# Two transformer layers on one core: output-side matmuls issued as four 128x32 column tiles, with a re-made instruction order and staging buffers in reused memory

## The chip, the cores and the metric

The kernel runs on one core of one Trainium2 chip. The metric is device time in microseconds (us), lower is better. A core has a matmul engine (PE, whose weight loads are shown as PEld), a vector engine (DVE), an activation engine (ACT), a general engine (POOL) and a queue engine (SP) that starts every data transfer (DMA) here. Each engine runs its own instruction list in order; semaphores tie the lists together.

## The reference

The input is one sequence of 2048 tokens of width 576 in bf16. The reference applies this twice:

```python
x = x + _A_ref(_layernorm(x), wqkv, wo)
x = x + _B_ref(_layernorm(x), w1, b1, w2, b2)
```

`_A_ref` normalizes again, makes q, k and v (32 heads of width 18), and does attention in which a token sees itself and the 255 tokens before it; the result goes through `wo` (576 by 576):

```python
mask = (idx[:, None] - idx[None, :] >= 0) & (idx[:, None] - idx[None, :] < W)   # W = 256
p = _softmax(jnp.where(mask, q @ k.T * Dh ** -0.5, -1e9))
o = p @ v
return o.reshape(B, S, D) @ wo
```

`_B_ref` normalizes, multiplies by `w1` (576 by 4608), applies gelu with bias `b1`, and multiplies by `w2` (4608 by 576), plus `b2`.

## The kernel before

Work is cut into 8 chunks: 4 per layer, each of 4 tiles of 128 tokens. Chunk k passes through these stages.

- **Normalization.** DVE makes statistics (L678, L682), POOL the reciprocal root (L691, L693), DVE the normalized tile `xn` (L703), and, for a 64-wide remainder of the 576 columns, a second copy of it (L711, DVE). A transposing DMA (L727) then makes `xnTa` (for attention) or `xnTm` (for the MLP). `xn` is a ring of 3 slots.
- **q, k, v.** In chunks 0 and 1 each of q, k and v of a tile is two groups of five 128-row matmuls with 288 columns (`two_out`, L763). In later chunks the array is split into two halves of 64 rows (L803), two matmuls of 288 columns running beside each other. Results leave PSUM, the matmul output memory of 8 banks, by DVE casts (L811 for v, L824 for q and k). Chunk 1 may use bank 6 alone for this.
- **Attention.** Scores (L870) use four row tiles of 32 rows (one head each); ACT takes the exponential (L879), POOL zeroes what the mask forbids (L900), and the product with v (L917, `pv`) uses four column tiles: each matmul has 128 rows and 20 of 32 columns and writes its own 32 partitions of one bank. DVE then transposes and normalizes (L928, L931, L934, L938).
- **Output projection** (`tail`, again L763): ten 128x128 matmuls per token tile with 288 columns, then the residual add on DVE (L980), and normalization for the MLP.
- **First MLP matmul** (`G_part`, L1033): pairs of 64-row matmuls with 512 columns; ACT applies gelu (L1043).
- **Second MLP matmul** (`mm2`, L1071): the 36 blocks of 128 hidden columns are done in three parts of 12; for each token tile and each half of 288 output columns, 12 matmuls with a 128x128 stationary block of `hT` accumulate in one bank, and DVE adds the result into `x_res` (L980), or, in the last part of layer 2, writes the output tile to a slot of `xn` (L983), from which a DMA sends it out.

So four ways of using the array occur: whole (128x128), two row halves (64x128), four row tiles (32x128) and four column tiles (128x32).

The order of all instructions is set at build time by a list scheduler in the kernel (`Plan.schedule`): a task has a cost, a priority and an array mode ("f" whole, "h" halves, "r" row tiles, "c" column tiles), a switch of mode costs a fixed time in its model, `PL.turn` adds a preference against certain switches, and `PL.nudge` shifts the priority of each stage by a table of constants. Chunks are interleaved: while chunk k is in attention, chunk k-1 is in the MLP. The scheduler also puts filler matmuls on a zeroed tile (L665) into planned gaps of the first 140 us.

Weights `w1` and `w2` are streamed from DRAM again for each chunk, through a ring of three slots (`w1_sb`) and one buffer (`w2_sb`) that is refilled in two loads per part (six blocks each).

Of the kernel before, what the change touches and what calls it, by code (L numbers as in the profile page):

```python
# [159 lines left out]
class Task:  # L160
    __slots__ = ("idx", "eng", "fn", "reads", "writes", "cost", "lat", "prio", "dma", "ring", "handles", "alloc", "move", "desc",
                 "npred", "succ", "ready", "end", "plain", "fifo", "hold", "stage", "mode", "own")
# [24 lines left out]
class Plan:  # L187
# [21 lines left out]
    def add(self, eng, fn, reads=(), writes=(), dma=None, ring=4, cost=0.1, lat=0.1, prio=0.0, alloc=(), fifo=None, plain=False, after=(), move=0.0, desc=0, hold=False, mode="f", own=False):  # L209
        if eng == "dve" and fifo is None:  # L210
# [5 lines left out]
                 plain=plain, move=move, desc=desc, fifo=fifo, hold=hold, stage=stage, mode=mode, own=own)  # L216
# [31 lines left out]
    def keep_warm(self, a, b, bank_free, extra):  # L248

        if self.warm_fn is None or a < self.warm_from:  # L250
            a = max(a, self.warm_from)
        n = int((b - a - 0.1) * 0.8 / 0.115)
        banks = [x for x in (7, 6, 5, 4) if bank_free.get(x, 1e9) <= a]
        if n < 1 or not banks:
            return
        h = Bank(())
        h.no = banks[0]
        t = Task(idx=-1, eng="pe", fn=lambda e: self.warm_fn(e, h.no, n), reads=("warm",), writes=(h,), cost=n * 0.115, lat=0.1, prio=0.0,
                 dma=None, ring=4, alloc=(), handles=(), plain=False, move=0.0, desc=0, fifo=None, hold=False, stage="", mode="f", own=False)
        extra.append((a, t))  # L260

    def schedule(self):
        free = {e: BEGIN for e in ENGS}
        mode = "f"
        released = {e: [] for e in ENGS}
# [152 lines left out]
def build_kernel(nc, A_x, A_wqkv, A_wo, B_x, B_w1, B_b1, B_w2, B_b2, out):  # L418
# [26 lines left out]
    NXN = 3  # L445
# [14 lines left out]
    PL.turn = {"ff": 0.02, "fh": 0.24, "fc": 0.44, "rf": 0.05, "rr": 0.16, "cf": 0.56, "ch": 1.05, "cr": 0.47, "cc": 0.72}  # L460
    PL.nudge = {"": -255.24, "b": -219.8, "ea0.0": 23.65, "ea0.1": -0.79, "ea0.2": 6.45, "ea0.p0": -38.42, "ea0.p1": 20.22,
# [803 lines left out]
```

## Time and profile before

| what | us |
|---|---|
| median of 3 runs (lowest, highest) | 881.62 (880.4, 881.86) |
| the profiled execution, whole time | 880.89 |
| span of that execution, first to last instruction | 879.2 |
| PE idle before 24 us / from 24 to 95 us | 2.3 / 6.7 |
| PE idle from 95 to 800 us / after 800 us | 6.2 / 2.9 |

The granted PE clock was 1.000 throughout. PE idle is the length of a stretch less PE's busy time in it; busy time includes the modelled end of a matmul, so it is an upper bound of useful work. The last matmul group starts at 864.38 us and is followed by the last residual add (876.35 us) and the last output transfer.

### The profile page before, as it was taken

How to read it: one execution, taken by the hardware profiler on the slowest of the kernel's cores; microseconds unless marked ns; L12 is line 12 of the kernel's file. 1: busy time of each engine (PE TensorE's matmuls, PEld its weight loads, DVE VectorE, ACT ScalarE, POOL GpSimd, SP SyncE). 2: the span in 40 equal slices, each digit the busy share in tenths (PEclk: the TensorE clock that was granted, in tenths of full speed). 3: DMA queues.
4: the chain of work that ended last, by engine and by line, in shares of the span. 5: the costliest groups of instructions: out<-in, count | busy, mean ns of one | idle time of the engine just before them, and what ended most of it. 6: DMA issues, size and time to landing. Idle time of an engine off the chain costs nothing.

```text
span 879.2 us, 23104 instructions
## 1 busy us (share of the span) xinstructions
PE 861.2 (98%) x9675; PEld 507.4 (58%) x9675; DVE 414.2 (47%) x994; ACT 596.3 (68%) x741; POOL 367.8 (42%) x500
## 2 busy tenths in 40 slices
PE   9898999999999999999999999999999999999998
PEld 7444555556566565566655555655556555556665
DVE  6889423664237632476433943374233533262111
ACT  5976788858757696565774868729768589753443
POOL 3766554465234562254420845416444176231100
PEclk9999999999999999999999999999999999999999
DMA  7698435361585524936356262584425953445341
GB/s 193 141 196 187 113 114 135 110 165 52 163 164 126 136 63 157 181 108 179 103 131 186 62 180 84 150 174 111 155 82 136 226 123 104 136 130 171 104 159 50
DMA packets 181847, 119.53 MB, mean 136 GB/s; under 512 B 107440, under 2 KB 181744, under 8 KB 181744
## 3 DMA queue, kind: packets, MB, share of 16 engines
q1 hardware_dynamic: 181744, 118.05, 52.0%
q8 instruction: 77, 1.26, 0.6%
q14 instruction: 26, 0.21, 0.1%
HBM read 90.10 MB, written 2.36 MB: 105 GB/s over the span
## 4 chain that ended last, share of the span: by engine, by line
PE 80%; DVE 7%; DMA 4%; ACT 4%; issue 3%; POOL 2%; SPq 0%; DVEq 0%; POOLq 0%
PE ps L1033 31%; PE ps L1071 28%; PE ps L803 9%; PE ps L870 5%; PE ps L917 4%; PE ps L763 4%; ACT pT L879 3%; DVE xn L703 2%; DMA xnTm<-xn 2%; POOL pT L900 1%; DVE st_all L678 1%; DVE xn L711 1%; DMA xnTa<-xn 1%; DVE x_res L980 1%; ACT hT L1043 1%
## 5 line engine op out<-in xcount | busy, mean ns | idle before, releaser
L900 POOL TENSOR_SCALAR_AFFINE_SELECT pT<-pT 128x512 bf16<-128x512 bf16 (+1 forms) x368 | 287.8, 805 | 271.6 <-ACT pT L879 267.9
L879 ACT ACTIVATE pT<-ps 128x1024 bf16<-128x1024 f32 (+2 forms) x384 | 347.1, 972 | 51.5 <-PE ps L870 51.1
L1071 PE MATMUL ps<-w_sb,hT 128*128 128x288 bf16 x2208 | 298.5, 287 | 3.8 <-DVE x_res L980 2.0
L1043 ACT ACTIVATE hT<-ps,b1col 128x512 bf16<-128x512 f32 x276 | 168.4, 688 | 195.3 <-PE ps L1033 194.6
L1033 PE MATMUL ps<-xnTm,w_sb 64*128 64x512 bf16 x2592 | 292.8, 376 | 0.2 <-ACT pT L879 0.2
L1071 PEld LDWEIGHTS ps<-w_sb,hT 128*128 128x128 bf16 x2208 | 203.2, 98 | 84.6 <-issue 23.7
L1033 PEld LDWEIGHTS ps<-xnTm,w_sb 64*128 64x128 bf16 x2592 | 126.9, 94 | 141.9 <-issue 6.7
L980 DVE TENSOR_TENSOR x_res<-ps,x_res 128x288 f32<-128x288 f32 x224 | 99.1, 446 | 170.1 <-PE ps L1071 136.3
L928 DVE STREAM_TRANSPOSE oq<-ps 128x512 f32<-128x512 f32 x64 | 45.6, 712 | 112.1 <-PE ps L917 111.5
L803 PE MATMUL ps<-wqkv,xnTa 64*128 64x288 bf16 x1296 | 95.4, 283 | 2.5 <-DMA xnTa<-xn 0.9
L824 DVE CAST qn<-ps 128x288 bf16<-128x288 f32 x120 | 49.7, 449 | 80.6 <-PE ps L803 72.5
L803 PEld LDWEIGHTS ps<-wqkv,xnTa 64*128 64x128 bf16 x1296 | 61.1, 94 | 35.0 <-issue 6.4
L870 PE MATMUL ps<-qT,kT 32*128 32x384 bf16 (+2 forms) x1216 | 64.1, 276 | 2.0 <-ACT pT L879 1.7
L691 POOL TENSOR_SCALAR vtmp<-mv_all 128x1 f32<-128x1 f32 (+1 forms) x43 | 8.8, 206 | 130.6 <-DVE mv_all L682 129.1
L1049 POOL TENSOR_TENSOR x_res<-x_res,b2bc 128x576 f32<-128x576 f32 x32 | 40.7, 1293 | 43.8 <-ACT hT L1043 43.8
L678 DVE BATCH_NORM_STATS2 st_all<-x_res 128x6 f32<-128x288 f32 (+1 forms) x128 | 53.7, 443 | 1.7 <-DMA x_res<-in_A_x_dram 1.2
L917 PE MATMUL ps<-pT,vA 128*20 128x384 bf16 (+2 forms) x1408 | 50.4, 276 | 1.0 <-DVE qn L824 0.8
L703 DVE TENSOR_SCALAR xn<-x_res,mv_all,rstd 128x576 bf16<-128x576 f32 (+1 forms) x64 | 43.8, 685 | 13.8 <-DMA xnTm<-xn 5.7
L811 DVE CAST vA<-ps 128x288 bf16<-128x288 f32 x64 | 26.5, 448 | 40.5 <-PE ps L803 38.5
L763 PE MATMUL ps<-wo_sb,attT 128*128 128x288 bf16 x320 | 44.2, 287 | 0.6 <-DVE x_res L980 0.6
L870 PEld LDWEIGHTS ps<-qT,kT 32*128 32x128 bf16 x1216 | 19.4, 92 | 43.1 <-issue 30.3
L917 PEld LDWEIGHTS ps<-pT,vA 128*20 128x20 bf16 x1408 | 25.8, 90 | 23.1 <-issue 11.6
(47 smaller groups left out, 389.7 us busy)
## 6 DMA issues: line engine op xcount, KB each, us to landing
w_sb<-in_B_w_dram SPq DMA_DIRECT2D x48, 864.0 KB, 5.9
w_sb<-in_B_w_dram SPq DMA_DIRECT2D x48, 768.0 KB, 4.7
w_sb<-in_B_w_dram SPq DMA_DIRECT2D x96, 48.0 KB, 4.4
out_dram<-xn SPq DMA_DIRECT2D x16, 144.0 KB, 1.8
wqkv<-in_A_wqkv_dram SPq DMA_DIRECT2D x3, 576.0 KB, 5.3
x_res<-in_A_x_dram SPq DMA_DIRECT2D x3, 576.0 KB, 4.3
wo_sb<-in_A_wo_dram SPq DMA_DIRECT2D x4, 144.0 KB, 3.3
xnTm<-xn SPq DMA_TRANSPOSE x32, 2.6
```

Of the source, the lines that this page charges most:

```text
L678: add("dve", lambda e, i=i, s=s: e.bn_stats(st_all[:, t, i, :], s[:, t, i * HB:(i + 1) * HB]), reads=res, writes=[f"st{t}_{i}"], cost=0.37 ...
L703: add("dve", lambda e: e.tensor_scalar(xn[:, sl, 0:D], s[:, t, :], mv_all[:, t, 0:1], rstd[:, t:t + 1], op0=ALU.subtract, op1=ALU.mult), r ...
L763: ins = e.matmul(bank(bs[o])[:, 0:HB], lhs(c), rhs(c, o * HB), start=(c == 0), stop=(c == KD - 1))
L803: ins = e.matmul(bank(bs[o])[:, 0:HB], xnTa[r:r + 64, c, i * 128:(i + 1) * 128], wqkv[r:r + 64, c, col:col + HB], start=(c == 4), stop=(ph ...
L870: ins = e.matmul(two(bs[j // 2])[:, j % 2, col:col + nq * 128], k_of(T0 + so)[0][32 * j:32 * j + 32, g, :], qs[32 * j:32 * j + 32, g, qo * ...
L879: add("act", lambda e, h2=h2: e.activation(pT[:, sl, 2 * h2:2 * h2 + 2, lo:hi], two(bs[h2])[:, :, lo:hi], ACT.Exp, scale=SCALE), reads=[bs ...
L900: add("pool", lambda e, ap=ap, pat=pat, sgn=sgn, kind=kind: e.affine_select(ap, ap, pattern=pat, compare_op=(ALU.is_ge if kind == "d" else ...
L917: ins = e.matmul(bank(bo)[32 * j:32 * j + VW, qo * 128:(qo + nq) * 128], vA[:, (T0 + so) % VS, 8 * j + g, :], pT[:, sl, j, col:col + nq * ...
L980: add("dve", lambda e: e.tensor_tensor(x_res[:, t, sl], bank(b)[:, 0:HB], x_old[:, t, sl], ALU.add), reads=[b] + ([f"xin{t}"] if first els ...
L1033: ins = e.matmul(bank(bks[i])[:, 0:n], w1_sb[r:r + 64, sls[i], col:col + 128], xnTm[r:r + 64, k % 2, c, 0:n], start=(c == 4), stop=(ph == ...
L1043: add("act", lambda e, ff=ff, hd=hd, bk=bk: e.activation(hd[:, 0:n], bank(bk)[:, 0:n], ACT.Gelu_apprx_tanh, bias=b1col[:, ff:ff + 1]), rea ...
L1071: ins = e.matmul(bank(b)[:, 0:HB], h_of(k, hf, fl)[0][:, i * 128:(i + 1) * 128], w2_sb[:, fl, hh * HB:(hh + 1) * HB], start=(fl == 0), sto ...
```

## The change

1. A helper `quad` issues one 128x128 by 288 product as four matmuls, each with 32 columns of the stationary block, the same moving operand, and its own 32 output partitions. It replaces the single matmul in the second MLP matmul, in the output projection, and in chunk 1's q, k and v. The scheduler's mode of these tasks becomes "c".
2. The scheduler's constants change: `PL.turn`, the whole `PL.nudge` table, several task costs, and a rule that DVE's two normalizing operations and POOL's work exclude each other in the plan ("port"). So the order on every engine is new.
3. The second copy of the 64-wide remainder of `xn` moves from DVE (a second normalization) to POOL (a copy). The ring of `xn` grows from 3 to 4 slots.
4. Chunk 1's q, k and v may use banks 6 and 7 instead of 6 alone.
5. In the first chunk of each layer the three score units of a head hold 384, 384 and 384 columns instead of 384, 512 and 256.
6. Dead space: 12 of the 16 output tiles are staged in `x_res` of tiles that are finished; the last chunk's last part of `w2` is loaded over `wqkv`; `b1` arrives in a block of `hT`; the filler's zero tile is half as wide.

```diff
     GW = GS * 128
-    NXN = 3
+    NXN = 4
...
-    PL.turn = {"ff": 0.02, "fh": 0.24, "fc": 0.44, "rf": 0.05, "rr": 0.16, "cf": 0.56, "ch": 1.05, "cr": 0.47, "cc": 0.72}
+    PL.turn = {"hc": 0.3, "rh": 0.05, "rc": 0.05, "ch": 0.3}
...
                 for t in released[e]:
                     st = max(free[e], t.ready)
+                    if t.port:
+                        st = max(st, port)
...
+            if t.port:
+                port = st + t.cost
...
-    b1in = sb("b1in", [NF, P], BF16)
+    b1in = hT[0:NF, NFH - 1, 0:P]
+    x_out = x_res[:, :, 0:HB].bitcast(BF16)
...
-            reads=res + [f"mv{t}", f"rstd{t}"], writes=[f"xn{sl}"], cost=0.67 if src is None else 0.45, lat=0.14, prio=prio)
+            reads=res + [f"mv{t}", f"rstd{t}"], writes=[f"xn{sl}"], cost=0.5 if src is None else 0.37, lat=0.14, prio=prio, port=True)
...
-            add("dve", lambda e: e.tensor_scalar(xn[:, sl, D:KD * 128], s[:, t, 512:D], mv_all[:, t, 0:1], rstd[:, t:t + 1],
-                                                  op0=ALU.subtract, op1=ALU.mult),
-                reads=res + [f"mv{t}", f"rstd{t}"], writes=[f"xd{sl}"], cost=0.38, lat=0.14, prio=prio)
+            add("pool", lambda e: e.tensor_copy(xn[:, sl, D:KD * 128], xn[:, sl, 512:D]), reads=[f"xn{sl}"], writes=[f"xd{sl}"], cost=0.22, lat=0.1,
+                prio=prio)
...
+    w2_x = wqkv.rearrange("p c d -> p (c d)")[:, 0:NFH * D].rearrange("p (f d) -> p f d", d=D)
+    def w2_of(k, hf):
+        return (w2_x, "w2x") if k == NK - 1 and hf == NPT - 1 else (w2_sb, "w2s")
...
+    def quad(e, b, lhs, rhs, start, stop):
+        ins = None
+        for j in range(4):
+            ins = e.matmul(bank(b)[32 * j:32 * j + 32, 0:HB], lhs[:, 32 * j:32 * j + 32], rhs, start=start, stop=stop,
+                           tile_position=(0, 32 * j), skip_group_check=True)
+        return ins
...
                 for c in range(KD):
-                    ins = e.matmul(bank(bs[o])[:, 0:HB], lhs(c), rhs(c, o * HB), start=(c == 0), stop=(c == KD - 1))
+                    if mode == "c":
+                        ins = quad(e, bs[o], lhs(c), rhs(c, o * HB), c == 0, c == KD - 1)
+                    else:
+                        ins = e.matmul(bank(bs[o])[:, 0:HB], lhs(c), rhs(c, o * HB), start=(c == 0), stop=(c == KD - 1))
...
-                             wr, prio + 0.01 * n, after=dest, fill=(6,) if k == 1 else FILL)
+                             wr, prio + 0.01 * n, after=dest, fill=(6, 7) if k == 1 else FILL, mode="c" if k == 1 else "f")
...
+        if t0 == 0:
+            us = [[(0, 0, 3, 0)], [(1, 1, 3, 128)], [(2, 2, 2, 256), (3, 3, 1, 128)]]
...
+        elif outp[0] == "x":
+            add("dve", lambda e: e.tensor_tensor(x_out[:, t - 4, sl], bank(b)[:, 0:HB], x_res[:, t, sl], ALU.add),
+                reads=[b, f"x{t}h{hh}"], writes=[f"yo{t}h{hh}", f"x{t - 4}h0"], cost=0.375, lat=0.14, prio=prio)
...
-                         [f"aT{c}" for c in range(KD)] + [f"wo{x}{j}" for x in "AB" for j in range(4)], prio)
+                         [f"aT{c}" for c in range(KD)] + [f"wo{x}{j}" for x in "AB" for j in range(4)], prio, mode="c")
...
                         for fl in range(f0, f0 + 6):
-                            ins = e.matmul(bank(b)[:, 0:HB], h_of(k, hf, fl)[0][:, i * 128:(i + 1) * 128], w2_sb[:, fl, hh * HB:(hh + 1) * HB],
-                                           start=(fl == 0), stop=(fl == NFH - 1))
+                            ins = quad(e, b, h_of(k, hf, fl)[0][:, i * 128:(i + 1) * 128], wt[:, fl, hh * HB:(hh + 1) * HB],
+                                       fl == 0, fl == NFH - 1)
```

More of the change, by code (lines that the diff above doesn't have):

```diff
@@ L161 @@
     __slots__ = ("idx", "eng", "fn", "reads", "writes", "cost", "lat", "prio", "dma", "ring", "handles", "alloc", "move", "desc",
-                 "npred", "succ", "ready", "end", "plain", "fifo", "hold", "stage", "mode", "own")
+                 "npred", "succ", "ready", "end", "plain", "fifo", "hold", "stage", "mode", "own", "port")
     def __init__(self, **kw):
@@ L207, in __init__, with add @@
         self.fifo_last = {}
-    def add(self, eng, fn, reads=(), writes=(), dma=None, ring=4, cost=0.1, lat=0.1, prio=0.0, alloc=(), fifo=None, plain=False, after=(), move=0.0, desc=0, hold=False, mode="f", own=False):
+    def add(self, eng, fn, reads=(), writes=(), dma=None, ring=4, cost=0.1, lat=0.1, prio=0.0, alloc=(), fifo=None, plain=False, after=(), move=0.0, desc=0, hold=False, mode="f", own=False, port=None):
         if eng == "dve" and fifo is None:
@@ L215, in add @@
                  dma=dma, ring=ring, alloc=tuple(alloc), handles=tuple({r for r in tuple(reads) + tuple(writes) if isinstance(r, Bank)}),
-                 plain=plain, move=move, desc=desc, fifo=fifo, hold=hold, stage=stage, mode=mode, own=own)
+                 plain=plain, move=move, desc=desc, fifo=fifo, hold=hold, stage=stage, mode=mode, own=own,
+                 port=(eng == "pool" and dma is None) if port is None else port)
         pred = set()
@@ L258, in keep_warm @@
         t = Task(idx=-1, eng="pe", fn=lambda e: self.warm_fn(e, h.no, n), reads=("warm",), writes=(h,), cost=n * 0.115, lat=0.1, prio=0.0,
-                 dma=None, ring=4, alloc=(), handles=(), plain=False, move=0.0, desc=0, fifo=None, hold=False, stage="", mode="f", own=False)
+                 dma=None, ring=4, alloc=(), handles=(), plain=False, move=0.0, desc=0, fifo=None, hold=False, stage="", mode="f", own=False, port=False)
         extra.append((a, t))
@@ L264, in schedule @@
         mode = "f"
+        port = 0.0
         released = {e: [] for e in ENGS}
@@ L655, in zero @@
         for c in range(2):
-            ins = e.matmul(bank(b)[:, c * 256:(c + 1) * 256], warm[:, 0:128], warm[:, :], start=True, stop=True)
+            ins = e.matmul(bank(b)[:, c * 256:(c + 1) * 256], warm[:, :], warm[:, :].unsqueeze(1).to_broadcast([P, 2, P]), start=True, stop=True)
         return ins
@@ L664, in warm_fn @@
         for _ in range(n):
-            ins = e.matmul(bank(bk)[:, 0:256], warm[:, 0:128], warm[:, :], start=True, stop=True)
+            ins = e.matmul(bank(bk)[:, 0:256], warm[:, :], warm[:, :].unsqueeze(1).to_broadcast([P, 2, P]), start=True, stop=True)
         return ins
@@ L746, in w1_load, with w2_load, two_out @@
                 lat=1.4, move=0.17, desc=64, prio=prio)
-    def w2_load(hf, prio, gate=None):
+    w2_x = wqkv.rearrange("p c d -> p (c d)")[:, 0:NFH * D].rearrange("p (f d) -> p f d", d=D)
+    def w2_of(k, hf):
+        return (w2_x, "w2x") if k == NK - 1 and hf == NPT - 1 else (w2_sb, "w2s")
+    def w2_load(hf, prio, gate=None, k=0):
+        wt, wn = w2_of(k, hf)
         for b in range(NFH // WB):
             f0 = hf * NFH + WB * b
-            dma("sp", w2_sb[:, WB * b:WB * b + WB, :], B_w2[f0 * P:(f0 + WB) * P, :].rearrange("(w p) d -> p w d", p=P),
-                reads=[gate[b]] if gate else [], writes=[f"w2s{b}"], cls="w2", ring=NFH // WB, cost=0.55, lat=2.0, move=0.44 * WB,
+            dma("sp", wt[:, WB * b:WB * b + WB, :], B_w2[f0 * P:(f0 + WB) * P, :].rearrange("(w p) d -> p w d", p=P),
+                reads=[gate[b]] if gate else [], writes=[f"{wn}{b}"] + ([f"w{w}{x}{h}" for w in "qkv" for x in "BC" for h in range(2)] + [f"w{w}A" for w in "qkv"] if wn == "w2x" else []), cls="w2", ring=NFH // WB, cost=0.55, lat=2.0, move=0.44 * WB,
                 desc=128 * WB, prio=prio)
-    def two_out(lhs, rhs, reads, prio, after=(), fill=FILL):
+    def quad(e, b, lhs, rhs, start, stop):
[4 more added lines that the diff above has]
+        return ins
+    def two_out(lhs, rhs, reads, prio, after=(), fill=FILL, mode="f"):
         bs = [Bank(fill), Bank(fill)]
@@ L762, in fn @@
                 for c in range(KD):
-                    ins = e.matmul(bank(bs[o])[:, 0:HB], lhs(c), rhs(c, o * HB), start=(c == 0), stop=(c == KD - 1))
+                    if mode == "c":
+                        ins = quad(e, bs[o], lhs(c), rhs(c, o * HB), c == 0, c == KD - 1)
+                    else:
+                        ins = e.matmul(bank(bs[o])[:, 0:HB], lhs(c), rhs(c, o * HB), start=(c == 0), stop=(c == KD - 1))
                 return ins
-            add("pe", fn, reads=reads, writes=[bs[o]], cost=mm_cost(HB) * KD, lat=0.22, prio=prio, alloc=[bs[o]], after=after)
+            add("pe", fn, reads=reads, writes=[bs[o]], cost=mm_cost(HB) * KD, lat=0.22, prio=prio, alloc=[bs[o]], after=after, mode=mode)
         return bs
@@ L934, in pv @@
         add("dve", lambda e: e.tensor_tensor(attq[:, 0:4 * nt, g * DH:(g + 1) * DH], oq[:, 0:4 * nt, 0:DH], rb, ALU.mult),
-            reads=["oq", f"ri{r}"], writes=[f"aq{g}"], cost=0.6, lat=0.14, prio=prio - 3)
+            reads=["oq", f"ri{r}"], writes=[f"aq{g}"], cost=0.4, lat=0.14, prio=prio - 3, port=True)
         for c in range(KD):
@@ L981, in resid @@
                 reads=[b] + ([f"xin{t}"] if first else []), writes=[f"x{t}h{hh}"] + over, cost=0.375, lat=0.14, prio=prio, own=first and hh == 1)
-        else:
-            add("dve", lambda e: e.tensor_tensor(xn[:, outp, sl], bank(b)[:, 0:HB], x_res[:, t, sl], ALU.add),
-                reads=[b, f"x{t}h{hh}"], writes=[f"xn{outp}" if hh == 0 else f"xd{outp}"], cost=0.375, lat=0.14, prio=prio)
+        elif outp[0] == "x":
+            add("dve", lambda e: e.tensor_tensor(x_out[:, t - 4, sl], bank(b)[:, 0:HB], x_res[:, t, sl], ALU.add),
+                reads=[b, f"x{t}h{hh}"], writes=[f"yo{t}h{hh}", f"x{t - 4}h0"], cost=0.375, lat=0.14, prio=prio)
+        else:
+            sn = int(outp[1:])
+            add("dve", lambda e: e.tensor_tensor(xn[:, sn, sl], bank(b)[:, 0:HB], x_res[:, t, sl], ALU.add),
+                reads=[b, f"x{t}h{hh}"], writes=[f"xn{sn}" if hh == 0 else f"xd{sn}"], cost=0.375, lat=0.14, prio=prio)
     def tail(k, prio):
@@ L1044, in G_part @@
                                                                       bias=b1col[:, ff:ff + 1]),
-                    reads=[bk, "b1"], writes=[hn] + ([f"p{fl // 4}{x}" for x in ("h0", "h1", "m0", "m1", "m2")] if hn[1] == "p" else []), cost=0.145 + n * 0.00087, lat=0.17,
+                    reads=[bk, "b1"], writes=[hn] + ([f"p{fl // 4}{x}" for x in ("h0", "h1", "m0", "m1", "m2")] if hn[1] == "p" else []), cost=0.125 + n * 0.00087, lat=0.17,
                     fifo="act", prio=prio)
@@ L1057, in mm2 @@
         l, t0, nt = CH[k]
+        wt, wn = w2_of(k, hf)
         for i in range(nt):
@@ L1061, in mm2 @@
             PL.part = f".{i}"
-            if fin:
-                osl = xn_ctr[0] % NXN
+            osl, wait = None, []
+            if fin and t >= 4:
+                osl, odst, ord_ = f"x{t}", x_out[:, t - 4, :], [f"yo{t}h0", f"yo{t}h1"]
+            elif fin:
+                sn = xn_ctr[0] % NXN
                 xn_ctr[0] += 1
+                osl, odst, ord_ = f"n{sn}", xn[:, sn, 0:D], [f"xn{sn}", f"xd{sn}"]
+                wait = ord_
             for hh in range(2):
@@ L1070, in fn @@
                         for fl in range(f0, f0 + 6):
-                            ins = e.matmul(bank(b)[:, 0:HB], h_of(k, hf, fl)[0][:, i * 128:(i + 1) * 128], w2_sb[:, fl, hh * HB:(hh + 1) * HB],
-                                           start=(fl == 0), stop=(fl == NFH - 1))
-                        return ins
-                    add("pe", fn, reads=[h_of(k, hf, fl)[1] for fl in range(f0, f0 + 6 if f0 or i + hh == 0 or k == NK - 1 and i < 2 else NFH)] + [f"w2s{f0 // WB}"], writes=[b],
-                        cost=6 * mm_cost(HB), lat=0.22, prio=prio + 0.05 * i, alloc=((b,) if f0 == 0 else ()),
-                        after=([f"xn{osl}", f"xd{osl}"] if fin and f0 == 0 else ()))
-                resid(t, hh, b, prio, outp=(osl if fin else None))
+                            ins = quad(e, b, h_of(k, hf, fl)[0][:, i * 128:(i + 1) * 128], wt[:, fl, hh * HB:(hh + 1) * HB],
+                                       fl == 0, fl == NFH - 1)
+                        return ins
+                    add("pe", fn, reads=[h_of(k, hf, fl)[1] for fl in range(f0, f0 + 6 if f0 or i + hh == 0 or k == NK - 1 and i < 2 else NFH)] + [f"{wn}{f0 // WB}"], writes=[b],
+                        cost=6 * mm_cost(HB), lat=0.22, prio=prio + 0.05 * i, alloc=((b,) if f0 == 0 else ()), mode="c",
+                        after=(wait if f0 == 0 else ()))
+                resid(t, hh, b, prio, outp=osl)
             if fin:
-                dma("sp", out_dram[t * P:(t + 1) * P, :], xn[:, osl, 0:D], reads=[f"xn{osl}", f"xd{osl}"], cls="o", ring=4, cost=0.5,
+                dma("sp", out_dram[t * P:(t + 1) * P, :], odst, reads=ord_, cls="o", ring=4, cost=0.5,
                     prio=prio)
@@ L1120, in build_kernel @@
         cost=0.5, prio=-1)
-    add("pe", lambda e: e.transpose(bank(bb).bitcast(BF16)[:, 0:NF], b1in[:, :], ident[0:NF, 0:NF]), reads=["b1i", "ident"], writes=[bb],
+    add("pe", lambda e: e.transpose(bank(bb).bitcast(BF16)[:, 0:NF], b1in, ident[0:NF, 0:NF]), reads=["b1i", "ident"], writes=[bb],
         cost=0.1, lat=0.22, prio=5, alloc=[bb])
```

8 lines of the change are left out of this document (4 added, 4 removed), and 141 rows, old and new, of the table add.

## The prediction, made before the changed kernel was run

> **What bounds the kernel now.** I read the page's busy times first, then the matmul engine by stretches, the timeline of a long stretch of pure MLP work, the timeline of an interleaved stretch, and the table of waits.
>
> ```profile
> PE 861.2 (98%) x9675; PEld 507.4 (58%) x9675; DVE 414.2 (47%) x994; ACT 596.3 (68%) x741; POOL 367.8 (42%) x500
> 24.00:95.00 71.00, 64.31 (x813) 34.15 (x812) 61.81 (x156) 54.16 (x69) 47.29 (x67) 1.00 0.84 172
> 600.00:700.00 100.00, 100.00 (x1176) 57.79 (x1175) 38.50 (x90) 74.20 (x90) 42.66 (x54) 1.00 0.54 144
> ```
>
> The first line is the page's, the others are two stretches (from:to, length, then busy time of PE, PEld, DVE, ACT, POOL). PE is busy 98% of the span and without a hole between 600 and 700 us; only from 24 to 95 us is another engine nearly as full (DVE 61.8 of 71). So time comes down only if PE's own work shrinks, or in the early stretch. Is a busy PE streaming? Pure MLP work first (start, length, engine, line, operation, count):
>
> ```profile
> 805.36 15.71 PE L1033 MATMUL ps<-xnTm,w_sb 64*128 64x512 bf16 x144
> 821.01 11.93 PE L1071 MATMUL ps<-w_sb,hT 128*128 128x288 bf16 x96
> 832.87 7.94 PE L1033 MATMUL ps<-xnTm,w_sb 64*128 64x512 bf16 x72
> ```
>
> From start to start, 72 pairs of first-MLP matmuls take 15.65 us and 96 second-MLP matmuls 11.86 us. Now interleaved work:
>
> ```profile
> 526.61 1.64 PE L1071 MATMUL ps<-w_sb,hT 128*128 128x288 bf16 x12
> 528.18 0.40 PE L870 MATMUL ps<-qT,kT 32*128 32x384 bf16 x8
> 528.51 1.65 PE L1071 MATMUL ps<-w_sb,hT 128*128 128x288 bf16 x12
> 530.09 0.40 PE L870 MATMUL ps<-qT,kT 32*128 32x384 bf16 x8
> 530.41 0.83 PE L917 MATMUL ps<-pT,vA 128*20 128x384 bf16 x24
> 531.18 0.91 PE L1071 MATMUL ps<-w_sb,hT 128*128 128x288 bf16 x6
> ```
>
> Twelve matmuls and one score unit, 526.61 to 528.51, take 1.90 us. Let s be the price of a change of array mode. A second-MLP matmul is (11.86 - s)/96 and a 512-column group (15.65 - s)/72; with s near 0.1 these are 122.5 ns and 216 ns. So 1.90 holds 12 x 0.1225 = 1.47 and 0.216 (a score unit streams 384 + 128 columns), and leaves 0.21 for two switches: 0.105 each. With 0.01 us rounding and a second small group in the score unit I take s = 0.095, ends 0.09 and 0.11. The weight-load lane shows the same thing as idle time that nothing in the profile explains ("issue"; total us, times, longest):
>
> ```profile
> PEld ps L870 <- issue: 34.7, 144, 0.4
> PEld ps L1071 <- issue: 23.7, 112, 0.4
> PEld ps L917 <- issue: 11.6, 50, 0.4
> PEld ps L1033 <- issue: 6.7, 28, 0.5
> ```
>
> That sum exceeds the price, since a load normally runs ahead of its matmul; it tells where the switches are, not what they cost.
>
> **The change part by part.**
>
> *Fewer switches.* I counted changes of mode along PE's list in the built programs. Before there are 518: 191 into and 191 out of score units, 64 between whole array and halves, 23 between halves and columns, 49 between whole and columns. After there are 412: 192 into and 192 out of scores, 26 between halves and columns, one each of the two whole-array kinds. The other two joins vanish because the second MLP matmul, the projection and the product with v now share a mode; scores still switch. 106 x 0.095 = -10.1 us, nearly all on PE's path since PE is 98% busy (ends -9.5 to -11.7).
>
> *The price of a quad.* 2304 second-MLP, 320 projection and 120 chunk-1 matmuls become 2744 quads, 4 x 2744 = 10976 matmuls with as many weight loads. If a quad takes what the whole matmul took, this costs nothing; break-even with the saving is 10.1/2744 = 3.7 ns a quad, 3% of 122.5. This is the crux. No row has 32-column tiles with 288 columns. The nearest is the product with v, the same tiling with 20 columns:
>
> ```profile
> 32.40 0.67 PE L917 MATMUL ps<-pT,vA 128*20 128x384 bf16 x16
> 33.00 0.29 PE L870 MATMUL ps<-qT,kT 32*128 32x256 bf16 x4
> 184.34 0.14 PEld L917 LDWEIGHTS ps<-pT,vA 128*20 128x20 bf16 x8 [0.25 <-issue]
> 184.37 0.34 PE L917 MATMUL ps<-pT,vA 128*20 128x384 bf16 x4
> ```
>
> The unit at 32.40 (16 matmuls: groups of 384, 384, 128 and 256 columns) takes 0.60 us to the next start, the one at 530.41 (24 matmuls, 1536 columns) 0.77 us. Both end in one switch, so it falls out of the difference: 384 more columns in two more groups cost 0.17 us, which for 288 columns is 0.1275, or 0.120 if rounding took 0.01 us off, and it holds two groups' fixed cost where a quad has one. That is the whole matmul's 122.5 ns within what the stamps can tell. I take a difference of 0, ends -2 ns (-5 us) and +5 ns (+14 us).
>
> What might break the parallel is the number of instructions: a quad is 8 (four loads, four matmuls) per 122.5 ns, 15.3 ns each, for hundreds in a row, where before it was two. The 24-matmul unit above ran 48 instructions in 0.77 us, 16 ns each, but its matmuls also had 1536 columns to stream. The last two lines of the fence, from a stretch that ends at 184.40, show 8 loads and 4 matmuls begun within 0.06 us of a drain, 5 ns each; they may have been made ready while PE stood waiting, so this bounds a short burst and not a long run. Instruction bytes roughly double (queue 8 of the page: 77 packets, 1.26 MB), which its 0.6% share of the transfer engines can bear.
>
> [...]
>
> *The early stretch.* PE idles 6.7 us from 24 to 95 us. Part of it is chunk 1's casts out of its single bank:
>
> ```profile
> PE ps L763 <- DVE qn L824: 1.4, 4, 0.7
> PE ps L763 <- DVE vA L811: 1.0, 2, 0.7
> ```
>
> (waits of PE in that stretch). A second bank lets the next group of five run while DVE casts the last, and moving the second copy away takes 11 instructions, 4.8 us, off DVE there (L711's busy time in that stretch). I take -2.0 of these 2.4 us; ends -4 (other waits on DVE too) and +3 (bank 7 is also where the product with v lands, and the order is new).
>
> *The second copy on POOL.* 60 copies leave DVE (L711, 28.0 us in all) and join POOL; nearest POOL rows: a 128x256 clear 0.31 us (L645), a one-column operation 0.20 (L691), so about 15 us on an engine 42% busy. A copy can stand behind a mask step of 1.15 us (L900, large form); late next is its transposing DMA on SP, and behind that on the same queue the weight loads. Cover: no wait of PE for weights is in the table of waits, and waits for `xnTa` come to 0.9 us. I take 0, ends 0 and +2.
>
> *At nothing:* the t0 = 0 score units (32 exponentials of 1024 columns at 1.025 us and 32 of 512 at 0.605 become 64 of 768 at 0.810: 52.2 to 51.8 us, ACT is 68% busy); the same counts of mask steps; six fewer fillers, which stand in gaps; the `b1` transfer into `hT`, unused until the first gelu; outputs from `x_res` and the moved `w2` loads (two of 48, same sizes), since PE has no wait after 800 us that they could remove. The end after the last matmul is the same chain: residual add 0.46 us, output transfer 1.8 us.
>
> *The new order.* All waits move. PE's idle from 95 to 800 us is 6.2 us in a few holes; a new order could close or add some: 0, ends -4 and +5.
>
> *Sum* against the profiled execution (880.9, span 879.2 plus 1.7 around it): 880.9 - 10.1 - 2.0 = 868.8. That execution lies 0.7 below the median shown, so for a median I say 869.
>
> **The rivals.**
>
> *Quads paced by their instructions (slower).* Place: the quad runs of 48 and more matmuls. Price: at 16 ns an instruction, the pace of the 48-instruction unit, a quad takes 128 ns, +5.5 x 2744 = +15: 884. It decides from 12.1/2744 = 4.4 ns a quad. For: the unit's pace coincides. Against: its columns alone explain that pace, and 12 instructions began in 0.06 us.
>
> *Waits take half the saving.* ACT is 68% busy and DVE 87% early; PE arriving sooner waits for exponentials or gelus (L879 and L1043 already end some PE waits). Half of 12 lost: 875.
>
> *Switch without gain.* Going from 20-column tiles to 32-column tiles could drain the array all the same. There are 67 such joins in the new list (40 and 27): 67 x 0.095 = +6.4: 875. Against: nothing in a group differs but the number of columns.
>
> *More than forecast.* If the early stretch loses 4 and the later holes 4, with switches at 0.11: 880.9 - 11.7 - 8 = 861.
>
> **How the numbers follow.** Forecast 869 (own range 864 to 874): 0.58. Waits take half: 0.11. Switch without gain: 0.04. More than forecast: 0.05. Quads paced by instructions: 0.18, of which a third is beyond 886 and the rest lies between no change and there. No change, where these cancel: 0.04. A measurement of this kernel can tell about 0.2%, 1.8 us, from no change. Faster: 0.58 + 0.11 + 0.04 + 0.05 = 0.78; waits that take more than half move 0.01 of it to no change and 0.02 to slower: 0.75, 0.05, 0.20. The range 861 to 886 leaves out about 0.03 below and 0.1 above.
>
> **What would show it.** Right: pure second-MLP stretches at the end still take near 11.8 us per 96 products; "issue" idle ahead of the second MLP's loads stays only where scores or halves come before; PE's waits for L811 and L824 early shrink; about 869. Wrong: 96 products take 12.2 us or more (instruction pace), or PE busy falls by 10 us while the span doesn't (waits), or "issue" idle stands between the product with v and a quad.

## The result, and the profile after

| | us |
|---|---|
| before, median of 20 runs (lowest, highest) | 881.43 (880.09, 883.79) |
| after, median of 20 runs (lowest, highest) | 879.61 (874.72, 883.14) |
| ratio, 95% interval | 0.9974 [0.9961, 0.9986] |
| the profiled execution after: whole time, span | 880.96, 879.3 |

Faster by 1.8 us where 12 were forecast. The profiled execution lies above the median, and its span equals that of before (879.2); what it shows is where a gain of some 10 us was spent again. First the lines that answer to those of before: the page's busy times, and two stretches (from:to, length, busy time of PE, PEld, DVE, ACT, POOL, then granted clock, share of the transfer engines, GB/s).

```profile
PE 856.9 (97%) x17901; PEld 543.0 (62%) x17901; DVE 394.1 (45%) x934; ACT 594.7 (68%) x741; POOL 378.0 (43%) x560
```

```profile
24.00:95.00 71.00, 62.25 (x1259) 36.57 (x1257) 55.57 (x143) 52.28 (x66) 50.14 (x81) 0.95 0.96 172
600.00:700.00 100.00, 96.82 (x1992) 59.58 (x1992) 33.69 (x73) 72.05 (x87) 41.73 (x51) 0.98 0.60 151
```

PE has twice the instructions and is *less* busy: 62.25 instead of 64.31 early, and 96.82 of 100 where it had no hole before. The clock, 1.00 before, is below it in both stretches. The timeline of PE at the end and near 690 us:

```profile
829.05 11.94 PE L768 MATMUL ps<-w_sb,hT 128*32 128x288 bf16 x384
840.92 11.83 PE L1058 MATMUL ps<-xnTm,w_sb 64*128 64x512 bf16 x108
...
689.48 0.83 PE L938 MATMUL ps<-pT,vA 128*20 128x384 bf16 x24
690.14 3.11 PE L768 MATMUL ps<-w_sb,hT 128*32 128x288 bf16 x96
696.32 0.61 PE L891 MATMUL ps<-qT,kT 32*128 32x384 bf16 x8 [3.07 <-DMA qT<-qn]
```

96 products as quads take 11.87 us from start to start, as the 11.86 of before. Over the whole trace a quad's period (start to start, steps over 140 ns left out) is 123.1 ns, the whole matmul's of before 123.3. The 24-matmul product with v takes 0.66 us to the quad behind it, where it took 0.77 to a whole matmul: that join no longer switches. So both main steps of the forecast hold. But in the last line PE stands for 3.07 us. The waits of PE (total us, times, longest), before and then after:

```profile
PE ps L870 <- ACT pT L879: 2.3, 5, 0.9
PE ps L1071 <- DVE x_res L980: 2.0, 3, 0.9
...
PE ps L803 <- DMA xnTa<-xn: 0.9, 1, 0.9
```

```profile
PE ps L891 <- DMA qT<-qn: 4.4, 3, 3.1
PE ps L768 <- issue: 3.3, 6, 0.9
PE ps L891 <- issue: 2.3, 2, 1.8
...
PE ps L822 <- DMA xnTa<-xn: 1.4, 2, 1.0
PE ps L891 <- DMA kT<-qn: 1.2, 1, 1.2
PE ps L891 <- ACT pT L900: 1.1, 5, 0.3
```

Summed over all such rows, waits for DVE fell from 9.0 to 4.0 us and for ACT from 4.0 to 1.1: the new order did well. Waits for DMA rose from 1.1 to 7.3, and "issue", where nothing in the profile explains the wait, from 0 to 5.9. The longest of these, 1.8 us, is a DMA too: PE's semaphore instruction stands 2.27 us there, until a transposing DMA lands. All but 0.3 us of the others are like this one:

```profile
55.38 1.04 PE L768 MATMUL ps<-wqkv,xnTa 128*32 128x288 bf16 x25
57.18 0.67 PE L768 MATMUL ps<-wqkv,xnTa 128*32 128x288 bf16 x15 [0.77 <-issue]
```

Here PE stops inside one task, between two matmuls of one accumulation, with operands there and no semaphore between them. Numbering PE's instructions in the trace, I find eight such stops of over 0.2 us beyond the normal step (5.25 us in all, the largest 1.03). Counted modulo 256 instructions, all stand at the same place, give or take one; before has none. One packet of the instruction queue (16,384 bytes each), a block from here on, goes with 256 of them: PE's 36,107 loads, matmuls and semaphore instructions are 141.0 times 256, and the queue has 141 packets; before's 19,657 are 76.8 times 256, and it has 77. The DMA rows of before and after (packets, MB, share; or issues and median us to landing):

```profile
q1 hardware_dynamic: 181744, 118.05, 52.0%
q8 instruction: 77, 1.26, 0.6%
...
qT<-qn SPq DMA_TRANSPOSE x28, 3.3
...
kT<-qn SPq DMA_TRANSPOSE x26, 3.4
```

```profile
q1 hardware_dynamic: 181744, 118.05, 55.1%
q8 instruction: 141, 2.31, 1.0%
...
qT<-qn SPq DMA_TRANSPOSE x28, 4.2
...
kT<-qn SPq DMA_TRANSPOSE x26, 4.3
```

The data are the same bytes but need more time, and the transposing DMAs of q and k land 0.9 us later (those of the normalized rows 0.4). Last, two stretches behind long waits:

```profile
68.20:75.00 6.80, 6.02 (x74) 3.47 (x78) 2.41 (x6) 3.03 (x4) 1.80 (x3) 0.50 1.02 274
...
696.30:699.60 3.30, 3.28 (x56) 1.97 (x60) 0.00 (x0) 1.94 (x2) 0.61 (x1) 0.50 1.07 351
```

The granted clock is 0.5 for 6.83 and 3.41 us, and quads there follow each other at 240 ns instead of 123; at that rate PE's 6.02 + 3.28 busy us would have been half of that, so as an estimate about 4.7 us are lost. The windows follow stands of PE of 1.8 and 3.1 us.

**The supply, from the trace.** For each 256th PE instruction of after, counted so that the stops are among them, I took the time to the start of the next packet on the instruction queue. In 125 of 141 cases one begins within 4 us; in nearly all others the packet had begun before, by up to 1.8 us. Of the 125, where the 16 transfer engines were less than 20% busy in the microsecond that follows, it begins 0.6 us later on average (62 cases), where they were over 90% busy 1.7 us (40 cases), at most 3.83; ahead of the eight stops it took 1.9 to 3.5 us. The transfer takes 1.0 us, and PE resumed 1.3 to 1.6 us after its end. Together that is, as an estimate, about 3 us in quiet and 4 to 6 us among data, and 256 instructions of quads last 3.9 us. In the kernel before 7 blocks also began over 2 us late, without a stop: there the 256 instructions ahead of them last 7 to 11 us. That a block is asked for when PE enters the one before is inferred from this; no row of the profile names the request.

My theory, then: quads cost nothing in the array but need a block of instructions every 3.9 us; among data transfers this comes late (direct stops), and the blocks themselves delay transposing DMAs (waits, and half clock behind them). The rivals: the new order is worse than it looks, or quads cost something everywhere.

### The profile page after: what moved, and what is told of

Read it like the earlier page. It is cut to its first block, busy times and chain, and to the rows that moved or that the text cites. A ratio compares the mean times of both kernels' runs of the same rounds, so it can differ in the third digit from the quotient of the medians.

```text
span 879.3 us, 39623 instructions
## 1 busy us (share of the span) xinstructions
PE 856.9 (97%) x17901; PEld 543.0 (62%) x17901; DVE 394.1 (45%) x934; ACT 594.7 (68%) x741; POOL 378.0 (43%) x560
## 4 chain that ended last, share of the span: by engine, by line
PE 90%; DMA 5%; DVE 2%; issue 1%; ACT 1%; POOL 1%; SPq 0%; DVEq 0%; POOLq 0%
PE ps L768 36%; PE ps L1058 32%; PE ps L822 9%; PE ps L891 6%; PE ps L938 4%; DMA qT<-qn 2%; DMA xnTa<-xn 1%; DMA xnTm<-xn 1%; PE ps L782 1%; ACT pT L900 1%; PE ps L669 1%; DMA xnTm<-qn 1%; DMA kT<-qn 1%; POOL pT L921 0%; SPq L619 0%
## 5 line engine op out<-in xcount | busy, mean ns | idle before, releaser
L921 POOL TENSOR_SCALAR_AFFINE_SELECT pT<-pT 128x512 bf16<-128x512 bf16 (+1 forms) x368 | 282.6, 789 | 316.5 <-ACT pT L900 312.1
L900 ACT ACTIVATE pT<-ps 128x1024 bf16<-128x1024 f32 (+1 forms) x384 | 346.7, 971 | 82.3 <-PE ps L891 81.4
L768 PE MATMUL ps<-w_sb,hT 128*32 128x288 bf16 x8448 | 288.4, 287 | 1.9 <-issue 1.3
L1058 PE MATMUL ps<-xnTm,w_sb 64*128 64x512 bf16 x2592 | 288.3, 376 | 1.0 <-DVE st_all L682 0.4
L768 PEld LDWEIGHTS ps<-w_sb,hT 128*32 128x32 bf16 x8448 | 216.8, 97 | 54.1 <-issue 21.3
L822 PE MATMUL ps<-wqkv,xnTa 64*128 64x288 bf16 x1296 | 91.7, 286 | 1.8 <-DMA xnTa<-xn 1.4
L768 PE MATMUL ps<-wo_sb,attT 128*32 128x288 bf16 x1280 | 44.0, 294 | 1.2 <-issue 1.2
L768 PEld LDWEIGHTS ps<-wo_sb,attT 128*32 128x32 bf16 x1280 | 34.0, 99 | 10.4 <-issue 3.7
L707 DVE TENSOR_SCALAR xn<-x_res,mv_all,rstd 128x576 bf16<-128x576 f32 (+1 forms) x64 | 37.1, 593 | 7.2 <-DMA xnTm<-xn 6.1
L938 PEld LDWEIGHTS ps<-pT,vA 128*20 128x20 bf16 x1408 | 27.6, 91 | 19.2 <-issue 6.3
```

The source lines that it names most:

```text
L768: ins = e.matmul(bank(b)[32 * j:32 * j + 32, 0:HB], lhs[:, 32 * j:32 * j + 32], rhs, start=start, stop=stop, tile_position=(0, 32 * j), sk ...
L822: ins = e.matmul(bank(bs[o])[:, 0:HB], xnTa[r:r + 64, c, i * 128:(i + 1) * 128], wqkv[r:r + 64, c, col:col + HB], start=(c == 4), stop=(ph ...
L900: add("act", lambda e, h2=h2: e.activation(pT[:, sl, 2 * h2:2 * h2 + 2, lo:hi], two(bs[h2])[:, :, lo:hi], ACT.Exp, scale=SCALE), reads=[bs ...
L921: add("pool", lambda e, ap=ap, pat=pat, sgn=sgn, kind=kind: e.affine_select(ap, ap, pattern=pat, compare_op=(ALU.is_ge if kind == "d" else ...
L938: ins = e.matmul(bank(bo)[32 * j:32 * j + VW, qo * 128:(qo + nq) * 128], vA[:, (T0 + so) % VS, 8 * j + g, :], pT[:, sl, j, col:col + nq * ...
L1058: ins = e.matmul(bank(bks[i])[:, 0:n], w1_sb[r:r + 64, sls[i], col:col + 128], xnTm[r:r + 64, k % 2, c, 0:n], start=(c == 4), stop=(ph == ...
```

## Experiments

All change only how tasks are issued, or one task's place or engine; the planner's order stays that of its kernel. "Work" is PE's matmul work done so far, in us of streaming, so that the same amount means the same place in every kernel; all kernels have 791.

**No quads (a_whole).** Each quad is issued as one 128x128 matmul, in the order of after: 478 switches instead of 412.

```diff
-        for j in range(4):
-            ins = e.matmul(bank(b)[32 * j:32 * j + 32, 0:HB], lhs[:, 32 * j:32 * j + 32], ...
+        return e.matmul(bank(b)[:, 0:HB], lhs, rhs, start=start, stop=stop, ...
```

> The changed kernel's order on every engine, word for word, but each quad is issued as one 128x128 matmul again. In this order that makes 478 changes of array mode instead of 412 (+66 x 0.095 = +6.3 us), and PE's list shrinks from 35.8 to 19.3 thousand loads and matmuls. Supply theory (the changed kernel loses about 5.6 us in nine holes that lie exactly 256 instructions, or multiples of it, apart on PE's list, because the list is not fetched as fast as quads eat it): the holes go, +6.3 - 5.6, about 880 us (878 to 882.5), and no hole at those places. Rival (quads cost nothing beyond their columns, and the missing gain went to late transposes alone): +6.3, about 886.

870.23 us, ratio 0.9862 [0.9839, 0.9885], with 76 instruction packets and no stop at a block's end. The order and the other edits are worth 11.3 us without any quad; with 66 switches fewer, worth 6.3, quads should have made 864 of it, and made 879.6. They cost 15.7 us here. Both figures expected were far too high: the supply theory had counted the stops alone, and they are a third of the cost.

The half-clock windows can't be much of the rest. The granted clock on record tells the executions that had none (1.000) from those that had: a_whole's two without took 868.8 and 869.1 us (its two with one 871.4 and 871.8), after's two without 875.4 and 879.9. Between these the distance is 8.7 us on average, against 9.4 in the medians.

**Quads before's way (b_quads).** Quads in the order of before, otherwise untouched: 476 switches instead of 518.

> The kernel before, its order on every engine unchanged, with every second-MLP, projection and chunk-1 product issued as a quad. Mode changes fall from 518 to 476 (-42 x 0.095 = -4.0 us); PE's list grows from 19.4 to 35.8 thousand. Supply theory: holes of 4 to 7 us appear in it: 881 to 885 against 881.4. Rival (quads are free): -4.0, about 877.4, and no holes.

891.58 us, 1.0113 [1.009, 1.0137]: 10 slower where 42 fewer switches give -4. 141 packets, qT lands after 4.2 us, kT after 4.4, one half-clock window of 3.41 us. So the cost belongs to the quads, not to the new order. It is again more than the stops: the time is 6.6 us above the range expected, and the stops at block ends come to 3.1 us. PE's waits for DVE rose most, from 9 to 16.6 us in all. Behind the two longest (2.4 and 2.2 us) stand late transposing DMAs: for those that must have read a slot of `xn` before it is written again, DVE waited 7.8 us in all in before and 16.9 us here.

**Quads only where they save a switch (a_join).** Column runs that hold no product with v are issued whole, since they stand between scores and switch either way. 796 of 2744 quads remain, and 412 switches.

```diff
+            if not any(".p" in x.stage for x in run):
+                for x in run:
+                    x.fn = as_whole(x.fn)
```

> The changed kernel's order, but quads stay only in those unbroken column-tile runs that hold a product with v; all other second-MLP, projection and chunk-1 products are one 128x128 matmul. 796 of 2744 quads remain, the number of mode changes stays 412, PE's list falls to 24.1 thousand loads and matmuls. Supply theory: most of the 5.6 us of holes goes: about 874.5 us (873 to 877). Rival (holes have another cause, quads are free): no change, 879.6.

868.82 us, 0.9856 [0.9833, 0.9879], 4 us below the range expected: more went with the quads than their stops. 95 packets, stops at block ends 0.3 us. Its profiled execution (872.27, the slowest of its runs) shows what is left:

```profile
PE ps L914 <- DMA qT<-qn: 5.3, 2, 4.1
PE ps L961 <- POOL pT L944: 2.1, 2, 1.3
PE ps L845 <- DMA xnTa<-xn: 2.0, 1, 2.0
```

The 4.1 us wait is the one near 690 us.

**The moved w2 load (a_w2late).** SP's queue in after, near that wait:

```profile
688.91 0.37 SPq L619 DMA_DIRECT2D wqkv<-in_B_w_dram  x1
689.38 1.67 SPq L862 DMA_TRANSPOSE qT<-qn  x1
```

An 864 KB load into `wqkv`, which exists since the change, is issued just ahead of the transposing DMA that PE waits for. Here it is put behind it:

```diff
+        late = [x for x in order if "w2x0" in x[1].writes and x[1].dma == "w2"]
+        order = [x for x in order if x is not late[0]]
+        at = max(i for i, x in enumerate(order) if x[1].dma == "t" and any(w[0] == "q" for w in x[1].writes))
+        order.insert(at + 1, late[0])
```

> The changed kernel with two neighbours swapped on SP's list: the first load of w2 over the dead wqkv is issued behind the last transposing DMA of q instead of ahead of it. Theory (that load delays the transpose, PE waits 3.1 us for it near 693 us and then runs 3.4 us at half clock): -3 to -5 us, about 875. Rival (the transpose waits for the other weight loads ahead of it in any case): within 1 us of 879.6.

878.82 us, 0.9967 [0.9954, 0.998]. The wait is gone:

```profile
690.52 3.11 PE L773 MATMUL ps<-w_sb,hT 128*32 128x288 bf16 x96
693.57 0.40 PE L896 MATMUL ps<-qT,kT 32*128 32x384 bf16 x8
```

From 620 to 640 us of work it takes 22.7 us instead of 26.5. A part is lost again elsewhere: the profiled execution is 2.2 us ahead of after's, the median 0.8. That is the rival's figure, though not for its reason, since the wait did go. The load matters, but it isn't the main cause.

**Both (c_joinlate)**, a_join with this load moved:

> a_join with the first w2 load that was moved (the 864 KB one into wqkv) issued behind the last transposing DMA of q, as in a_w2late. Instruction supply and late transposes: the block count stays at 95 packets and 412 switches; PE's hole of 4.4 us near 690 us and the half-clock window behind it go, so 865 us (863 to 867), about 4 below a_join's 868.8. Rival, the prediction's own step that the moved loads cost nothing: 869, as a_join.

866.29 us, 0.9831 [0.9818, 0.9843], in the range expected; 2.5 below a_join. **Without quads (d_wholelate)** the load's place does nothing:

> c_joinlate without any quad: a_whole with the first moved w2 load behind the last transposing DMA of q. a_whole's trace has no hole near 690 us, so if that load only matters where transposes come late, 870 us, as a_whole (870.2), and c_joinlate's 66 switches fewer are worth 4 us net of its 796 quads. Rival, the load's place is worth 2 us or more in itself: 868 or below.

870.03 us, 0.9862 [0.9846, 0.9877]. So 796 quads that save 66 switches are worth 3.7 of the 6.3 us, and the load hurts only where the transposing DMA is late already.

**Where quads stand (d_quiet, d_busy).** The decisive pair. c_joinlate gets quads in half of its whole column runs: those during which data transfers filled at most 12% of the transfer engines (982 quads, 57 runs), or the others (966 quads, 55 runs).

```diff
+            no += len(run) > 0
-            if not any(".p" in x.stage for x in run):
+            if no not in quads and not any(".p" in x.stage for x in run):
```

> c_joinlate (quads only in the column runs that hold a product with v: 796 of 2744) with quads added in 57 more of its column runs, 982 quads, namely those during which the data transfers filled at most 12% of the transfer engines in the trace of a_w2late; the other 55 runs stay whole. 412 switches as in c_joinlate and d_busy. Theory: a block of 256 instructions is asked for when PE begins the one before, and its transfer waits behind the data's; quads hurt where data are on the way. So here hardly a hole at multiples of 256 instructions (below 1 us in all), late transposes only a little, 868 us (866 to 870). Rival, each quad costs the same wherever it stands: half way between c_joinlate's 866.3 and a_w2late's 878.8, 872.5, as d_busy.

> The mirror of d_quiet: quads added to c_joinlate in the 55 other runs, 966 quads, during which the data transfers filled more than 12% (mostly over half) of the transfer engines; the 57 quiet runs stay whole. Nearly the same number of instructions as d_quiet. Theory: holes at multiples of 256 instructions of 2 to 4 us in all, transposes later, 876 us (873 to 879). Rival, each quad costs the same wherever it stands: 872.5, as d_quiet.

d_busy took 877.12 us, 0.9943 [0.9928, 0.9958]. d_quiet took 866.9 us (864.4 to 867.4 in four of its five executions), 0.9821 [0.9805, 0.9838]. e_quiet is the same kernel:

> d_quiet once more, for a trace (its first profiled execution took 4855 us, every engine slowed throughout, and shows nothing of the kernel). Theory: 866 to 868 us; below 1 us of holes at multiples of 256 instructions although its instruction queue moves as many blocks as d_busy's 118; the transposing DMAs near c_joinlate's median. Rival, the time agrees but for another reason: holes of 2 us or more at the block ends, made up elsewhere.

865.98 us, 0.9827 [0.9805, 0.9849]. Both have 118 packets on the instruction queue. PE's longest waits in d_busy, then in e_quiet:

```profile
PE ps L855 <- DMA xnTa<-xn: 2.9, 3, 1.0
PE ps L801 <- issue: 2.6, 3, 1.2
PE ps L1091 <- DMA xnTm<-xn: 2.3, 1, 2.3
PE ps L924 <- DMA kT<-qn: 2.1, 2, 1.6
...
PE ps L924 <- issue: 1.3, 1, 1.3
```

```profile
PE ps L855 <- DMA xnTa<-xn: 2.3, 1, 2.3
PE ps L924 <- DMA qT<-qn: 1.5, 2, 1.2
```

The same number of blocks, the same 412 switches, and 11 us between them. 982 quads in quiet stretches cost nothing over c_joinlate (866.3), 966 among data cost 10.8 us. Stops at block ends are 0.25 us in e_quiet and 3.1 in d_busy; waits for DMA 4.9 and 8.8. The rival that a quad costs the same everywhere (872.5 for both) is out. All of PE's waits come to 10.6 us in e_quiet and 20.8 in d_busy, which accounts for the distance; beside the two kinds named, those for DVE rise from 4.0 to 6.5. The two sets of runs also differ in where they lie: 13 of the busy ones are before 110 us, none of the quiet ones. But by the table below the distance arises behind that.

**Half the instructions (c_pairs, c_joinpairs).** Two tiles of 64 columns instead of four of 32, in all products and in those of c_joinlate.

```diff
-        for j in range(4):
+        for j in range(2):
-            ins = e.matmul(bank(b)[32 * j:32 * j + 32, 0:HB], lhs[:, 32 * j:32 * j + 32], rhs, ...
+            ins = e.matmul(bank(b)[64 * j:64 * j + 64, 0:HB], lhs[:, 64 * j:64 * j + 64], rhs, ...
```

> Each group of four 128x32 tiles becomes two 128x64 tiles, four instructions for 288 columns where the quads have eight. Supply: some 98 packets on the instruction queue, no hole of PE at multiples of 256 instructions since 256 of them now last 7.9 us and not 3.9, transposes later by a third of what the quads make them. If 64-column and 20-column tiles follow each other without a switch (412 switches) 867 us, if they pay it (67 more) 873. Rival, tiles side by side have a cost of their own that goes with their number rather than their instructions' supply: half way from a_whole's 870.2 to the quads' 879.6, 875, with holes left.

> c_joinlate with pairs of 128x64 tiles in place of its quads. Supply: some 82 packets, no hole at multiples of 256 instructions, the hole near 690 us gone: 862 us if 64-column and 20-column tiles follow each other without a switch, 868 if the 67 joins pay 95 ns each. Rival, the quads of a_join are few enough to cost nothing in supply: then pairs win nothing over c_joinlate, the same 865, or lose the joins, 871.

c_pairs took 879.45 us (0.9977 [0.9967, 0.9988]), c_joinpairs 872.39 (0.9895 [0.9882, 0.9908]). As the supply theory had it, neither stops at a block's end. The joins with the 20-column tiles do pay: 67 of them at a median of 96 ns. So pairs have the switches of whole matmuls and gain nothing. But c_pairs is 6 us above my figure for that case, c_joinpairs 4: against a_whole c_pairs has 5.1 us more of holes, among them a wait of 2.4 us for a statistic on DVE at 87 us with a half-clock window behind it, and a pair's period is 124.17 ns against the whole matmul's 123.22, 2.6 us in all. The transposing DMAs land later by 0.13 us on average over all 120, a third of the 0.36 of quads, as expected. Why the rest arises I haven't settled: a part of what small tiles cost may lie outside the supply of instructions, and this run speaks neither for nor against the late blocks.

**The second copy (c_dvecopy).** a_whole with the 60 copies on DVE instead of POOL, at the same places.

> a_whole with the 60 second copies of the normalized rows run on DVE, at the same place in the order, not on POOL. The prediction's step: the copy on POOL costs nothing on PE's path (0, end +2), so 870.2 within 2 us, down at most. Rival: POOL's copy is what saved DVE in the early stretch, so DVE is later there and the time rises by 1 to 2 us, 872; the transposes of the normalized rows would show it between 24 and 95 us.

875.04 us, 0.993 [0.9913, 0.9948], and 872.9 to 879.0 from run to run. In its profiled execution, the slowest, it loses 1.6 us on a_whole up to 620 us of work, and 4.8 from there to 640, in the wait of the transposing DMA near 690 us again (2.81 us, with a half-clock window). Both figures expected are too low; the rival is nearer than my step's mere zero, and POOL's copy is a gain. The five executions without a half-clock window take 874.7 us on average, so that window isn't what makes the difference to a_whole.

The time at equal work (us), which shows where each kernel wins or loses:

| work | before | after | a_whole | c_joinlate | e_quiet | d_busy |
|---|---|---|---|---|---|---|
| 40 | 61.9 | 61.6 | 60.3 | 60.2 | 59.9 | 60.9 |
| 100 | 132.2 | 134.3 | 129.7 | 129.5 | 131.2 | 131.0 |
| 620 | 695.0 | 691.0 | 688.0 | 682.8 | 683.4 | 689.4 |
| 640 | 717.4 | 717.5 | 709.9 | 705.3 | 705.2 | 712.8 |
| 788 | 872.7 | 872.8 | 863.2 | 858.2 | 858.4 | 868.0 |

After loses 3.3 us to a_whole's pace between 40 and 100 (61.6 to 134.3 us in after), where the transfer engines are busy throughout up to 95 us, 66% over the whole stretch, and its longer half-clock window lies, and 4.6 between 620 and 640, the wait of 3.1 us and the window behind it. E_quiet and d_busy are level at 100, and 6 us apart at 620.

## Why the prediction was wrong

- **Fewer switches, -10.1: right.** Streaming goes at 2.4 columns per ns (512 columns take 216 ns, 288 take 123, so 224 more take 93). The step from one mode to the next, less the streaming time of the matmul before it, has a median of 98 ns in both traces. 106 fewer of them are 10.4 us, inside its ends.
- **A quad at parity: right in the array, wrong on the path.** 123.09 ns measured against 122.5 taken. Both rivals built on the array fell: quads are not paced at 128 ns, and joins of 20-column with 32-column tiles pay nothing (0.66 us for 1536 columns in four tiles, 0.64 of it streaming at 2.4 columns/ns). Yet quads cost 15.7 us, 5.7 ns each, past the upper end of +14 and past the 4.4 ns from which the slower rival decides. That this rival's price, +15, is so near is a coincidence: the pace it rests on isn't there. Nor is the loss that of the rival of waits, which looked at ACT and DVE; PE's waits for these fell from 13 to 5.1 us.
- **The step that failed** is one of those costed at nothing: "Instruction bytes roughly double (queue 8 of the page: 77 packets, 1.26 MB), which its 0.6% share of the transfer engines can bear." The share is indeed only 1.0% after. What counts is the delay of one block (1.7 us on average among data, up to 3.8, before a transfer of 1.0 us begins) against the 3.9 us that 256 instructions of quads last, and what a block does to the DMA beside it. An average share answers neither.
- **What a block does to a transposing DMA** can be read pairwise: a_whole and after issue the same 120 in the same order. Of those that met no block in a_whole and met one in after, 48, the landing is 0.88 us later on average; where nothing changed in this (63), the median difference is 0.00, and the nine that met one only in a_whole land 0.91 us earlier. The forecast's "late next" had only its own moved steps in view, not these.
- **"The moved w2 loads (two of 48, same sizes)" at nothing: wrong** with late transposes (2.5 us, c_joinlate), right without (d_wholelate). The reason given looked at PE's waits after 800 us; what mattered was which DMA stands behind the load on SP's queue.
- **Half clock: not in the forecast**, 4.7 us in the profiled execution by the estimate above, from windows of 6.83 and 3.41 us; a_whole's has one window of 3.41 us.
- **Early stretch -2.0, new order 0 with end -4: right or better.** PE's waits for chunk 1's casts (2.4 us before, in the stretch from 24 to 95 us) are 0.2 us in the same stretch of after, against 1.4 us (0.8 before) in which the product with v now waits for the same casts, probably since it shares bank 7; a_whole is 2.5 us ahead of before at 100 us of work; its 40 fewer switches are worth 3.8, which leaves some 5 for the order. This is what kept the sign right, and it was luck: the forecast had put the new order at 0, and without these 5 us the kernel would have been slower.
- **The second copy on POOL, 0:** no loss, as said; without it a_whole takes 4.8 us more (c_dvecopy).

So the account: forecast 869; order and early stretch 5 us better; quads 15.7 us worse; 879.6. How the 15.7 divides between direct stops (5.25 in the profiled execution), later DMAs and half clock is open, since a wait that one kernel has can vanish in the next run. Half clock alone was not taken away by an experiment; by the few executions that had none it is one or two of the 15.7 us.

The best versions beat both kernels: c_joinlate 866.3 and e_quiet 866.0 us, 1.7% below before, with quads only where they save a switch, or where data are quiet.

## What to carry to other kernels

When a change multiplies an engine's instructions, compare the time that 256 of them last (here 3.9 us) with the time that a block takes to come while data transfers run (here 4 to 6 us, by the estimate above), stage by stage; the mean share of the queue, 1.0% here, did not tell. Use the small-tile form only where it saves a change of mode and leave the large one elsewhere: here a third of the quads brought all of the switches. Before a load is moved, look at which DMA is issued behind it and who waits for that one.

## What the runs showed of the hardware that was not expected

- An instruction block of 16 KB lasts 1.0 us on the instruction queue. In most cases (125 of 141 in after) it begins after PE enters the block before it, by 0.6 us on average in quiet, by 1.7 us and up to 3.8 among data.
- A transposing DMA that meets such a block lands about 0.9 us later (48 pairs of a_whole and after).
- PE needs 96 ns from 64-column to 20-column tiles and back (the median of 67 joins in c_pairs), as between whole and column tiles (96 and 98 in before), and nothing from 32-column to 20-column tiles (0.66 us for 1536 columns in after, 0.64 of it streaming).
- A granted clock of 0.5 for 3.41 us, once for twice that, came behind stands of PE from 1.2 us (a_whole, c_joinlate) to 4.1 us (a_join), though not behind each: d_busy's of 2.3 us and b_quads' of 2.2 us had none.
